# A running sum over 768 steps: one chain of six chunks or two chains of three

## The chip, the cores and the metric

The kernel runs on one core of a Trainium2 chip. The core has TensorE (matmuls into PSUM banks; "PE" in the profile, its weight loads "PEld"), VectorE ("DVE"), ScalarE ("ACT"), GpSimd ("POOL") and SyncE ("SP", which issues the DMAs here). The metric is the device time of one execution in microseconds. Before the change three runs took 821.51, 821.87 and 823.55 us, median 821.87.

## The reference

A gated linear attention feeds two dense blocks. What the change touches is in the attention:

```python
mag = sqrt(a_re**2 + a_im**2)
scale = minimum(mag, 0.999) / (mag + 1e-6)
ar, ai = a_re * scale, a_im * scale
for t in range(768):                       # per batch (4) and head (8), state 48 x 48, complex
    S_re, S_im = ar[t]*S_re - ai[t]*S_im + outer(k[t], v[t]), ar[t]*S_im + ai[t]*S_re
    y[t] = q[t] @ S_re
x = y                                      # (4, 768, 384)
u = x + (relu(x^T @ w_tok1) @ w_tok2)^T    # dense 1: over time, then over channels
x = u + relu(u @ w_ch1) @ w_ch2
k = relu(mix(x, mu_k) @ w_k); out = sigmoid(mix(x, mu_r) @ w_r) * (k*k @ w_v)   # dense 2
```

The kernel does not step through time. The product of the factors up to step t is the exponential of a running sum of logarithms (the decay) and a rotation by a running sum of angles. Both running sums over the 768 steps are what is changed here.

## The kernel before

**Tiling.** Time is cut into six chunks of 128 steps (partitions), channels are 384 wide (8 heads of 48). X1, X2 and X3 hold all six chunks of a batch in fp32. The four batches go one after the other through `attention(b)` and `dense(b)`; batch 0's attention runs alone, with weight conversions beside it, and the attention of each later batch is emitted between the dense work of the one before.

**The order of the attention** is a string of words, SEQ0 for batch 0 (L32) and SEQ1 for batch 1. S, L, A and R are squares, logarithms, slopes and angles of a half (three chunks); B is 50 warming matmuls; `C3` is `sums(3)`, the running sum of the fourth chunk; `D0` is `decays(0)`, the exponentials of the first half's sums; T0 to T7 are the steps of a software pipeline over the chunks (scaling q and k, DMA transposes, score matmuls, state update, y). In the kernel before, batch 0 has `C0 C3 C1 C4 C2 D0 C5 D1`.

**A chunk's sum** (`products`, `add`). For the decay (operand X3, PSUM tag "u") and the angle (X2, tag "y") a triangle matmul (`tri32`, fp32, 128x384) sums within the chunk. What came before the chunk is added by a carry matmul (`last32`, 32 partitions) from a copy of the last row of the chunk before, which ScalarE puts into `carry32` (the tile CH). In batch 0 the kernel before runs two chains: chunks 0 to 2, and chunks 3 to 5. The fourth chunk starts the second chain with all-ones matmuls (`ones32`) over chunks 0, 1 and 2, for each of the two sums. The second chain has a carry buffer of its own, and each chain has its own pair of PSUM banks (`bank`: ps_1 for the first, ps_a for the second). Batch 1 runs one chain through all six chunks, with one bank for each sum. Batches 2 and 3 take other matmuls.

**A chunk's evacuation** (`sums`, after the yield): two ScalarE copies that round (X1 and a scratch tile, L468 and L470), and two VectorE operations that take the remainder (`rest`, and X2, L472 and L473); both read the PSUM bank. In the profile these operations have L334, the line of the helper that calls them; the matmuls of the attention have L479.

**The decays of a half** (`decays`): two ScalarE sigmoids of 128x1152 and two VectorE multiplies of 128x1152.

**Filler.** `keep_busy` puts ten small matmuls with low priority (offset -2000) behind each of the twelve sums of batch 0 (L487); `warm` puts 50 in front of them (L495). They keep TensorE at work and compute nothing that is used.

**Weights.** `weights_gen` loads weight pieces (L253, tile wst, two buffers) and splits each into two fp16 parts: three VectorE operations to decode (L264 to L266), one to round (L269, or ScalarE's L271), one for the remainder (L275). The next piece but one is loaded when a remainder is done. Pieces have low priority in batch 0's attention (offset -300) and high in the dense part (100).

**The order on the engines.** A planner orders the instructions of each engine before the run, by priority (the place in the program, with offsets: 100 for the sums' matmuls and carry copies, `P_PE`) and by its own estimates of when operands and engines come free. Within `attention(0)`, manual edges keep ScalarE's and VectorE's work in the program's order only in the steps T0 to T7.

Of the kernel before, what the change touches and what calls it, by code (L numbers as in the profile page):

```python
# [13 lines left out]
ACTF = mybir.ActivationFunctionType  # L14
# [4 lines left out]
C = H * D  # L19
NJ = S // 128  # L20
# [8 lines left out]
PRE, CHUNKS = 29.0, 51.7  # L29


SEQ0 = "S0 L0 S1 L1 B1 A0 R0 A1 R1 C0 C3 C1 C4 C2 D0 C5 D1 T0 T1 T2 T3 T4 T5 T6 T7"  # L32
SEQ1 = "S0 S1 L0 L1 A0 R0 A1 R1 C0 C1 C2 D0 C3 C4 C5 D1 T0 T1 T2 T3 T4 T5 T6 T7"

ORD0 = "f01 f11 b0 w0 q0 k0 e0 i2 v1 u0 m01 m11 h01 h11 x2 a0 l0"
# [63 lines left out]
def split_path(  # L99
# [13 lines left out]
    def behind(later, earlier):  # L113

        for x in later:
            for y in earlier:
                tc.add_manual_dep(x.ins, y.ins.name, no_sync, reason="issue order")
        return later
# [5 lines left out]
    ACT = nc.scalar.activation  # L124
# [13 lines left out]
    tri32 = [const.tile([128, 128], F32, name=f"tri32{i}") for i in range(2)]  # L138
    ones32 = [const.tile([128, 128], F32, name=f"ones32{i}") for i in range(2)]
    last32 = const.tile([128, 128], F32, name="last32")  # L140
# [25 lines left out]
    CH = const.tile([128, 7, C], F32, name="CH")  # L166
# [4 lines left out]
    X3 = const.tile([128, NJ, C], F32, name="X3")  # L171


    carry32 = [CH[:, 5:7], CH[:, 3:5]]

    x_hl = {}

# [147 lines left out]
    def attention(b):  # L325
# [3 lines left out]
        st, hl, at = {}, {}, [None]  # L329

        def chained(fn, last):

            def call(*a, **k):
                ins = fn(*a, **k)  # L334
                if b == 0 and at[0] is not None:
                    last[:] = behind([ins], last)
                return ins

            return call

        on_act, on_dve = [], []
        ACT = chained(nc.scalar.activation, on_act)
# [10 lines left out]
        def tmp2():  # L353
            return tmps.tile([128, 512], F32, tag="tmp", name="t2")[:, 0:C]
# [4 lines left out]
        def wide():  # L359
            return one.tile([128, 3, C], F32, tag="wide", name="wide")  # L360
# [40 lines left out]
        def bank(tag, J, shape):  # L401
            if b == 0 and J % 2:
                return ps_a.tile(shape, F32, tag={"u": "a0", "y": "a1"}[tag], name=tag)
            return ps_1.tile(shape, F32, tag=tag, name=tag)


        def parts(J):
            if J < NJ and not plain:
                hl[J] = two.tile([128, 4, C], F16, tag="hl", name="hl")
                for X, k, sc in ((X3, 0, 2.0 ** L_S), (X2, 2, 2.0 ** F_S / (2.0 * math.pi))):  # L410
                    ACT(hl[J][:, k], X[:, J], ACTF.Copy, scale=sc)
                    STT(hl[J][:, k + 1], X[:, J], sc, hl[J][:, k], op0=MUL, op1=SUB)

        acc = {}

        def add(J, o, ps, X):

            k = J // 3 if b == 0 else 0
            first = J == 3 * k
            with tc.high_priority(offset=P_PE):  # L420
                if plain:
                    for i in range(J if first else 0):
                        MM(out=ps, lhsT=ones32[o // 2], rhs=X[:, i], start=i == 0, stop=False)
                    MM(out=ps, lhsT=tri32[o // 2], rhs=X[:, J], start=J == 0 or not first, stop=first)
                    if not first:
                        MM(out=ps, lhsT=last32[96:128], rhs=carry32[k][96:128, o // 2], start=False, stop=True)
                    if J + 1 < NJ and J + 1 != 3 * k + (3 if b == 0 else NJ):
                        ACT(carry32[k][96:128, o // 2], ps[96:128], ACTF.Copy)
                    return


                if J > 0:
                    for i in range(2):
                        nc.tensor.matmul(out=ps, lhsT=anti, rhs=hl[J - 1][:, o + i], start=False, stop=True, skip_group_check=True)
                for i in range(2):
                    nc.tensor.matmul(out=ps, lhsT=tri, rhs=hl[J][:, o + i], start=J == 0 and i == 0, stop=True, skip_group_check=True)
# [1 line left out]
        both = ((X3, 0), (X2, 2))  # L438

        def products(J):  # L440
            k = J // 3 if b == 0 else 0
            if J == 0 or plain:
                for o, tag in ((0, "u"), (2, "y")):
                    acc[J, o] = bank(tag, k if at[0] is None else at[0], [128, C])
            else:
                for o in (0, 2):
                    acc[J, o] = acc[J - 1, o]
            if not plain:
                if J == 0:
                    parts(0)  # L450
                parts(J + 1)
            for X, o in both:
                last_mm.clear()
                add(J, o, acc[J, o], X)
                if b == 0:
                    keep_busy(N_FILL0)

        def sums(J):

            if J == 0 or b > 0 or J % 3:  # L460
                products(J)
            if b == 0 and J == 0:
                products(3)
            if J % 3 == 0:
                rest[J // 3] = wide() if b > 0 or J == 0 else R[:, 1024:1024 + 3 * C].rearrange("p (j f) -> p j f", j=3)
            yield 0.4 if plain else 1.3
            ps = [acc.pop((J, o)) if plain else acc[J, o] for o in (0, 2)]
            ACT(X1[:, J], ps[0], ACTF.Copy, bias=ROUND_L)  # L468
            r = tmp2()
            ACT(r, ps[1], ACTF.Copy, bias=ROUND)  # L470

            STT(rest[J // 3][:, J % 3], X1[:, J], ROUND_L, ps[0], op0=SUB, op1=SUB)  # L472
            STT(X2[:, J], r, ROUND, ps[1], op0=SUB, op1=SUB)  # L473
            yield 1.2
# [3 lines left out]
        def MM(**k):  # L478
            last_mm[:] = [nc.tensor.matmul(**k)]  # L479
            if b == 0:  # L480
                behind(last_mm, ahead)

        def keep_busy(n):

            with tc.high_priority(offset=-P_FILL):
                for _ in range(n):
                    ins = nc.tensor.matmul(out=h1_ps[1][:, C:512], lhsT=tri, rhs=tri, start=False, stop=False, skip_group_check=True)  # L487
                    behind([ins], last_mm)
# [240 lines left out]
        if b == 0:  # L729
            h1_ps.extend((ps_a.tile([128, C], F32, tag="a2", name="h1a"), ps_1.tile([128, 512], F32, tag="s", name="h1b")))  # L730
            nc.tensor.matmul(out=h1_ps[1], lhsT=tri, rhs=qk16["qh"][:, 0:4], start=True, stop=True)
        kinds = {"S": squares, "L": logs, "A": slopes, "R": angles, "C": sums, "D": decays, "T": step, "B": warm}
        for word in (SEQ0 if b == 0 else SEQ1).split():
            yield from kinds[word[0]](int(word[1]))
# [186 lines left out]
    def run(gen, got, want):  # L921

        while got < want:
            c = next(gen, None)
            if c is None:
                return float("inf")
            got += c
        return got
# [18 lines left out]
    def attentions():  # L947
        for b in range(1, B):
            yield from attention(b)
            done[0] = b  # L950
            yield 0.0

    ag, acc = attentions(), 0.0
    cg, seen_w = checks_gen(), 0.0
    for b in range(B):
# [5 lines left out]
        for cost in dense(b):  # L961
# [5 lines left out]
            if b + 1 < B:  # L967
                x = pos / 141.0
                acc = run(ag, acc, lo + (hi - lo) * (x + KINK[b] * x * (1.0 - x)))
# [207 lines left out]
def fused_kernel(tc, *args):  # L1177
    nc = tc.nc

    args = [words(x) if x.dtype == I64 else x for x in args]  # L1180
    with tc.tile_pool(name="flag", bufs=1) as pool:
        flag = pool.tile([1, 1], I32, name="flag")
        raw, args = args[:14], args[14:]
        split_path(tc, *args[:4], *raw[5:14], *args[4:], flag)
        bad = nc.values_load(flag[0:1, 0:1], min_val=0, max_val=1)
        with tc.If(bad != 0):
            general_path(tc, *raw, args[4], args[7])
# [53 lines left out]
```

## Time and profile before

| | |
|---|---|
| runs shown | 821.51, 821.87, 823.55 us |
| profiled execution | 825.2 us, its span 823.4 us |
| TensorE busy | 750.1 us (91%) |
| VectorE busy | 583.5 us (71%) |
| ScalarE busy | 520.7 us (63%) |
| GpSimd busy | 21.1 us (3%) |
| granted clock, mean | 0.97 |
| chain of waits by engine | PE 51%, ACT 18%, DVE 15%, DMA 11% |

Times in the profile are microseconds from the start of the span. A row of the timeline has start, duration, engine, line, operation, output and inputs, shape, and a count where several equal instructions are merged; an fp32 matmul has two records. In brackets stands how long the engine had been idle before, and what ended that. Consecutive operations overlap a little in the records, so the step from one start to the next is the better measure of what one costs.

### The profile page before, as it was taken

The numbers are of one execution on the slowest core, as the hardware profiler recorded it, in microseconds if no ns is written. First come the engines' busy times: TensorE is split into PE (matmuls) and PEld (weight loads), VectorE is DVE, ScalarE is ACT, GpSimd is POOL, SyncE is SP. The second block draws the span as 40 slices with busy tenths as digits, with TensorE's granted clock in tenths as the row PEclk, the third lists the DMA queues.
The fourth block names the chain that finished last, engine by engine and source line by source line (L and its number), as shares of the span: only waits on it lengthen the run. The fifth ranks groups of instructions, "written<-read, shape, count | busy, mean of one in ns | idle before, by whom it ended". The sixth has DMA issues, their size and how long they took to land.

```text
span 823.4 us, 15170 instructions
## 1 busy us (share of the span) xinstructions
PE 750.1 (91%) x6107; PEld 474.0 (58%) x6107; DVE 583.5 (71%) x1016; ACT 520.7 (63%) x988; POOL 21.1 (3%) x53
## 2 busy tenths in 40 slices
PE   0969879999998999999998899999999999999996
PEld 0559855455555655556665556566565666666553
DVE  3898979999998858877667556769675534484822
ACT  6785569767767988655658696556656533142742
POOL 3000000001000000000000000000000000010000
PEclk9986989999999999999999999999999999999998
DMA  8249983444754821161407501143406432867300
GB/s 271 76 98 227 197 278 116 129 149 129 201 123 104 192 72 49 58 135 27 97 1 149 153 1 39 58 91 46 94 10 88 81 106 54 273 199 262 114 29 33
DMA packets 137949, 94.92 MB, mean 115 GB/s; under 512 B 104592, under 2 KB 120208, under 8 KB 137872
## 3 DMA queue, kind: packets, MB, share of 16 engines
q1 hardware_dynamic: 137872, 93.88, 44.6%
q8 instruction: 50, 0.82, 0.4%
q14 instruction: 27, 0.22, 0.1%
HBM read 63.97 MB, written 4.72 MB: 83 GB/s over the span
## 4 chain that ended last, share of the span: by engine, by line
PE 51%; ACT 18%; DVE 15%; DMA 11%; issue 4%; SPq 1%; ACTq 0%; DVEq 0%
PE ps L738 23%; PE a L738 16%; PE y L479 4%; ACT X L334 4%; DVE X L334 4%; PE u L479 3%; PE sp L479 2%; DMA X<-by_time_a_re_dram 2%; ACT tmp L870 2%; DMA Rc<-kl 2%; DMA Rc<-kh 1%; DVE Wc L334 1%; DMA Rc<-ql 1%; ACT ps L903 1%; ACT ps L904 1%
## 5 line engine op out<-in xcount | busy, mean ns | idle before, releaser
L738 PEld LDWEIGHTS <-wc 128*128 128x128 f16 x1728 | 166.7, 98 | 116.1 <-issue 13.5
L738 PE MATMUL a<-g,wc 128*128 128x384 f16 x864 | 162.5, 327 | 0.0
L738 PE MATMUL ps<-uh,wc 128*128 128x384 f16 x576 | 157.2, 327 | 2.3 <-DVE ul L788 1.5
L738 PE MATMUL a<-wv,g 128*128 128x384 f16 x576 | 110.2, 327 | 3.0 <-ACT g L905 2.6
L479 PEld LDWEIGHTS <-Rc 96*128 96x128 f16 (+1 forms) x1416 | 82.9, 101 | 48.8 <-issue 10.4
L738 PE MATMUL ps<-xkh,wk 128*128 128x384 f16 x384 | 107.2, 331 | 1.5 <-DVE g L906 1.5
L831 ACT ACTIVATE g<-ps 128x384 f16<-128x384 f32 x96 | 46.5, 484 | 86.5 <-PE ps L738 86.1
L738 PE MATMUL ps<-ul,wc 128*128 128x384 f16 x288 | 94.3, 327 | 0.0
L832 DVE SCALAR_TENSOR_TENSOR g<-ps,g 128x384 f16<-128x384 f32 x96 | 53.1, 555 | 45.9 <-ACT g L831 45.7
L479 PE MATMUL sp<-Rc 96*128 96x128 f16 x504 | 60.1, 228 | 18.8 <-DMA Rc<-kh 6.0
L738 PEld LDWEIGHTS <-g 128*128 128x128 f16 x576 | 54.0, 98 | 38.5 <-ACT g L905 4.8
L738 PEld LDWEIGHTS <-wk 128*128 128x128 f16 x576 | 55.4, 98 | 35.5 <-issue 4.3
L479 PE MATMUL y<-CH,Rc 96*128 96x48 f16 (+1 forms) x912 | 63.2, 185 | 4.0 <-ACT Rc L334 2.2
L738 PE MATMUL ps<-xkl,wk 128*128 128x384 f16 x192 | 63.3, 330 | 0.0
L906 DVE TENSOR_TENSOR g<-ps,g 128x384 f16<-128x384 f32 x64 | 35.5, 554 | 37.2 <-ACT g L905 37.1
L903 ACT ACTIVATE ps<-ps 128x384 f32<-128x384 f32 x64 | 30.5, 477 | 34.0 <-PE ps L738 30.8
L334 DVE TENSOR_TENSOR Wc<-cs,X 128x768 f32<-128x768 f32 x48 | 45.0, 952 | 0.2
L334 ACT ACTIVATE X<-X 128x1152 f32<-128x1152 f32 x32 | 37.0, 1158 | 11.5 <-DMA X<-by_time_a_re_dram 10.0
L334 DVE TENSOR_TENSOR m<-sp,tri 128x512 f32<-128x512 f32 x48 | 32.6, 685 | 15.1 <-PE sp L479 15.1
L479 PE MATMUL u<-CH,kh 128*128 128x48 f16 x320 | 38.5, 190 | 4.8 <-ACT kh L334 4.8
L334 ACT ACTIVATE X<-X,col_c 128x1152 f32<-128x1152 f32 x32 | 40.1, 1252 | 0.8 <-DVE Rc L334 0.4
L738 PE MATMUL ps<-wr,xrh 128*128 128x384 f16 x144 | 37.1, 325 | 0.0
(212 smaller groups left out, 1378.9 us busy)
## 6 DMA issues: line engine op xcount, KB each, us to landing
wst<-in_moe_w_ch_dram SPq DMA_DIRECT2D x24, 768.0 KB, 4.4
CH<-in_qk_dram SPq DMA_DIRECT2D x18, 384.0 KB, 3.0
wst<-in_moe_w_tok_dram SPq DMA_DIRECT2D x8, 768.0 KB, 5.0
wst<-in_moe_w_k_dram SPq DMA_DIRECT2D x8, 768.0 KB, 4.7
wst<-in_moe_w_v_dram SPq DMA_DIRECT2D x8, 768.0 KB, 4.6
X<-by_time_a_re_dram SPq DMA_DIRECT2D x8, 576.0 KB, 4.9
X<-by_time_a_im_dram SPq DMA_DIRECT2D x8, 576.0 KB, 6.7
CH<-by_time_v_dram SPq DMA_DIRECT2D x24, 192.0 KB, 3.1
```

What stands on the lines that cost most here:

```text
L334: ins = fn(*a, **k)
L479: last_mm[:] = [nc.tensor.matmul(**k)]
L738: return [nc.tensor.matmul(out=ps, lhsT=lh[a_], rhs=rh[b_], start=start and n_ == 0, stop=stop and n_ == 2) for n_, (a_, b_) in enumerate( ...
L831: ACT(part[:, 0], ps, ACTF.Relu)
L832: last_ev[:] = [STT(part[:, 1], ps, 0.0, part[:, 0], op0=MAX, op1=SUB)]
L870: ACT(w[:, 0:N], z[:, 0:N], ACTF.Copy, scale=o[:, c:c + 1])
L903: ACT(ps, ps, ACTF.Relu)
L904: ACT(ps, ps, ACTF.Square, scale=2.0 ** (SQ_S // 2 - XK_S - WK_S))
L906: last_ev[:] = [TT(part[:, 1], ps, part[:, 0], op=SUB)]
```

## The change

In batch 0 the sums of all six chunks form one chain, in the order of the chunks, as in batch 1. The all-ones matmuls and the second carry buffer go. The PSUM banks alternate by chunk (even chunks ps_1, odd chunks ps_a) and not by chain. The decays of the first half stand in the program behind the third chunk's sums and in front of the fourth's; before, they stood behind the third chunk's and in front of the sixth's. Batches 1 to 3 get the same instructions as before.

```diff
-SEQ0 = "S0 L0 S1 L1 B1 A0 R0 A1 R1 C0 C3 C1 C4 C2 D0 C5 D1 T0 T1 T2 T3 T4 T5 T6 T7"
+SEQ0 = "S0 L0 S1 L1 B1 A0 R0 A1 R1 C0 C1 C2 D0 C3 C4 C5 D1 T0 T1 T2 T3 T4 T5 T6 T7"
...
-    carry32 = [CH[:, 5:7], CH[:, 3:5]]
+    carry32 = CH[:, 5:7]
...
         def add(J, o, ps, X):

-            k = J // 3 if b == 0 else 0
-            first = J == 3 * k
             with tc.high_priority(offset=P_PE):
                 if plain:
-                    for i in range(J if first else 0):
-                        MM(out=ps, lhsT=ones32[o // 2], rhs=X[:, i], start=i == 0, stop=False)
-                    MM(out=ps, lhsT=tri32[o // 2], rhs=X[:, J], start=J == 0 or not first, stop=first)
-                    if not first:
-                        MM(out=ps, lhsT=last32[96:128], rhs=carry32[k][96:128, o // 2], start=False, stop=True)
-                    if J + 1 < NJ and J + 1 != 3 * k + (3 if b == 0 else NJ):
-                        ACT(carry32[k][96:128, o // 2], ps[96:128], ACTF.Copy)
+                    MM(out=ps, lhsT=tri32[o // 2], rhs=X[:, J], start=True, stop=J == 0)
+                    if J > 0:
+                        MM(out=ps, lhsT=last32[96:128], rhs=carry32[96:128, o // 2], start=False, stop=True)
+                    if J + 1 < NJ:
+                        ACT(carry32[96:128, o // 2], ps[96:128], ACTF.Copy)
                     return
...
         def products(J):
-            k = J // 3 if b == 0 else 0
             if J == 0 or plain:
                 for o, tag in ((0, "u"), (2, "y")):
-                    acc[J, o] = bank(tag, k if at[0] is None else at[0], [128, C])
+                    acc[J, o] = bank(tag, J, [128, C])
...
         def sums(J):

-            if J == 0 or b > 0 or J % 3:
-                products(J)
-            if b == 0 and J == 0:
-                products(3)
+            products(J)
             if J % 3 == 0:
```

## Rows read from the trace of the kernel before

**Rows 1.** The page, part 1: busy time, share of the span, instructions.

```profile
PE 750.1 (91%) x6107; PEld 474.0 (58%) x6107; DVE 583.5 (71%) x1016; ACT 520.7 (63%) x988; POOL 21.1 (3%) x53
```

**Rows 2.** Stretches: length, then PE, PEld, DVE, ACT, POOL busy, granted clock, DMA.

```profile
25.00:50.00 25.00, 25.00 (x160) 15.50 (x159) 23.23 (x38) 19.74 (x37) 0.00 (x0) 1.00 0.32 96
50.00:70.00 20.00, 13.67 (x150) 12.34 (x148) 20.00 (x30) 12.44 (x26) 0.00 (x0) 0.60 0.78 169
70.00:80.00 10.00, 9.46 (x114) 8.86 (x114) 7.26 (x12) 5.29 (x9) 0.00 (x0) 0.61 1.12 222
...
140.00:260.00 120.00, 113.90 (x790) 64.46 (x789) 114.62 (x200) 91.09 (x179) 3.73 (x10) 1.00 0.50 136
```

**Rows 3.** The chain of waits: start, length, engine, what; 10 to 150 us.

```profile
39.77 0.56 DVE X L334
...
48.34 2.41 DVE X L334 x3
...
105.56 8.09 DMA wst<-in_moe_w_ch_dram
```

**Rows 4.** Timeline of TensorE, 25 to 52 us.

```profile
25.10 1.59 PE L479 MATMUL y<-X,tri 128*128 128x384 f32 x2
26.49 0.90 PE L479 MATMUL y<-X,ones 128*128 128x384 f32 x2
...
31.09 0.81 PE L479 MATMUL y<-X,tri 128*128 128x384 f32 x2
...
33.77 0.91 PE L479 MATMUL y<-CH,last 32*128 32x384 f32 x2
...
40.45 0.80 PE L479 MATMUL y<-CH,last 32*128 32x384 f32 x2
41.19 0.91 PE L479 MATMUL y<-X,tri 128*128 128x384 f32 x2
...
42.68 0.91 PE L479 MATMUL y<-CH,last 32*128 32x384 f32 x2
...
44.16 1.01 PE L495 MATMUL h1b<-warm,tri 128*128 128x128 f16 x15
45.01 6.86 PE L487 MATMUL h1b<-tri 128*128 128x128 f16 x120
```

**Rows 5.** Timeline of ScalarE, 34 to 47 us.

```profile
34.77 0.48 ACT L334 ACTIVATE CH<-y 32x384 f32<-32x384 f32 x1 [0.82 <-PE y L479]
...
41.17 1.26 ACT L334 ACTIVATE X<-X,col_c 128x1152 f32<-128x1152 f32 x1
...
42.43 0.47 ACT L334 ACTIVATE t<-y 128x384 f32<-128x384 f32 x1
...
44.27 0.49 ACT L334 ACTIVATE X<-u 128x384 f32<-128x384 f32 x1
...
45.02 1.26 ACT L334 ACTIVATE X<-X,col_c 128x1152 f32<-128x1152 f32 x1
```

**Rows 6.** Timeline of VectorE, 42 to 51 us.

```profile
42.27 0.96 DVE L265 SCALAR_TENSOR_TENSOR wf<-wst,wf 128x768 int32<-128x768 int32 x1
...
43.61 2.62 DVE L334 SCALAR_TENSOR_TENSOR X<-wide,X 128x1152 f32<-128x1152 f32 x2
46.15 0.55 DVE L334 SCALAR_TENSOR_TENSOR Rc<-X,u 128x384 f32<-128x384 f32 x1
...
47.08 2.62 DVE L334 SCALAR_TENSOR_TENSOR X<-Rc,X 128x1152 f32<-128x1152 f32 x2
49.61 1.14 DVE L334 SCALAR_TENSOR_TENSOR X<-qk,col_c,X 128x384 f32<-128x384 f32 x2
```

**Rows 7.** Timelines of VectorE and TensorE, around 114 us.

```profile
113.67 0.56 DVE L264 TENSOR_SCALAR wf<-wst 128x768 int32<-128x768 int32 x1 [3.86 <-DMA wst<-in_moe_w_ch_dram]
...
114.81 0.32 PE L738 MATMUL h1a<-xl,wt 128*128 128x384 f16 x1 [3.21 <-DVE xl L334]
```

**Rows 8.** Waits from 115 to 205 us: who for whom, total, times, longest.

```profile
PE u L479 <- DVE wide L334: 0.4, 1, 0.4
```

## The prediction

> **What bounds the kernel now.** The page comes first: TensorE is busy for 750.1 us of the 823.4 us span, 91% [rows 1]. That is an average, and the change touches one stage only, the running sums of batch 0, so the second view is the table of stretches. From 25 to 50 us, where the sums lie, TensorE shows no gap, VectorE is busy 23.23 us of 25.00, and the granted clock is 1.00; from 50 to 70 us VectorE is busy 20.00 of 20.00 and TensorE 13.67; from 140 to 260 us TensorE is busy 113.90 of 120.00 [rows 2]. So VectorE carries the start and TensorE the dense part behind it. What the start gains reaches the end as long as the dense part begins that much earlier: its matmuls are a fixed amount of work.
>
> The third view is the chain of waits. It leaves the sums before they end: at 39.77 it comes to a VectorE evacuation, and from there to the three pieces at 48.34 every piece of work is VectorE's [rows 3]. The reader is to see that TensorE, full as it looks, does not end this stage alone: VectorE's queue does, and it holds weight conversions (0.96 us at 42.27, for example, [rows 6]) beside the sums.
>
> **The matmuls.** The sums start at 25.10 and the last matmul of them gives way to filler at 44.16 [rows 4]: 19.06 us for 26 matmuls. Six of these go away, the all-ones ones by which the fourth chunk rebuilt the sum of three chunks. They and one triangle matmul among them stand from 26.49 to 31.09: seven in 4.60, so 0.66 each and 3.95 for six. Two carry matmuls of the fourth chunk are added; two take 1.48 (42.68 to 44.16). The four triangle matmuls of the second and fourth chunk ran in one row, 31.09 to 33.77, 0.67 each; in a chain each alternates with carry matmuls, where four matmuls take 2.97 (41.19 to 44.16), 0.74 each: 0.30 more. Sum: -3.95 + 1.48 + 0.30 = -2.17, rounded to **-2.15 us** [rows 4].
>
> Does the chain itself keep up? A carry matmul of 0.91 starts at 33.77, its copy runs on ScalarE from 34.77 for 0.48 [rows 4, 5]; so the next carry matmul of that chain may start at about 35.3, 1.5 us after the one before. A chunk's four matmuls take 2.97, and the two chains (decay and angle) alternate, so one chain's turn hides under the other's matmuls. Banks alternate by chunk after the change, so a triangle matmul waits for the chunk two back: last matmul, carry copy 0.48, evacuation copy 0.49, VectorE 0.55 [rows 5, 6], in all 1.5 us and some hand-over, against 3 us until the bank is wanted. The second carry buffer falls away at no cost, since only one chain is left. Batch 1 already runs this single chain, with one bank per quantity, and there one triangle matmul waited 0.4 us for a VectorE evacuation [rows 8]. Batches 1 to 3 compute as before.
>
> **The carry copies.** Two more on ScalarE, 0.48 each [rows 5]. They are hidden: ScalarE is busy 19.74 us of 25.00 in this stretch [rows 2].
>
> **The decays of the first half.** Now the last chunk's first VectorE evacuation starts at 46.15, though its input copy ended at 44.76 (44.27 + 0.49): the decay multiplies of the first half, 2.62 us from 43.61, stand in front of it [rows 5, 6]. With these done earlier the tail is ScalarE's: the copies of the sums from 44.27, the sigmoid at 45.02, ended at 46.28, then the two multiplies of the second half, 2.62 together, from about 46.3 instead of 47.08 [rows 5, 6]. **-0.80 us**.
>
> What it costs to have them in front: two sigmoids of 1.26 each (41.17 to 42.43 with what belongs to it), 2.5 us of ScalarE, and the 2.62 of VectorE, between the third chunk's evacuations and the fourth's. In the trace a sigmoid at 41.17 held back the copy of the angle sums to 42.43, though its matmul (0.80 from 40.45) had ended at 41.25 [rows 4, 5]: 1.2 us late, and nobody waited for it. After the change the sixth chunk's triangle matmuls want the fourth chunk's bank. By the periods above the second chunk's matmuls start at about 27.2 and the fifth chunk's end at 39.1. If both sigmoids and the fifth chunk's carry copies stand in front of the fourth chunk's copies, these run at 39.6 and 40.1, VectorE frees the first bank at 40.7, and TensorE waits 1.6. If the sigmoids fall into ScalarE's gaps, nothing. Below nothing is excluded for this item alone, since the gain of moving them is already counted. I take **+0.5**, nearer to nothing, because ScalarE has 5.26 us of idle in 25.00. The Trainium skill (PSUM — Partial Sum Buffer, Engine vs sequencer instructions) says that the ScalarE and VectorE queues are strict FIFO, which speaks against this change: by it alone a carry copy or an evacuation behind a sigmoid waits for all of it, and the sum would take the 1.6 in place of the 0.5. The late copy at 42.43 agrees with the rule [rows 5].
>
> **What is behind it on VectorE.** The sums' stretch would so end 2.95 - 0.5 = 2.45 us sooner, but VectorE's work in it stays: 23.23 us busy, 1.77 idle [rows 2]. At least 0.7 us of it, so one weight operation (0.96, as at 42.27 [rows 6]), must go behind the stretch, where VectorE has no idle until 70 us. Bounds: nothing, if it lands in the 2.74 us of idle between 70 and 80 or later [rows 2]; 2.9, if three such operations move in front of the steps of the first chunks. I take **+1.0**, one operation, the least that the balance wants. The moved decays issue no DMA, and no queue of SP or POOL is passed by them.
>
> **Further on.** At 105 to 115 us the last chunk's low half of x (VectorE) stands behind a weight conversion that waits 3.86 for its DMA; TensorE waits 3.21 for that x [rows 7]. The chain of waits goes through that DMA, 8.09 us from 105.56 [rows 3]. It is issued when an earlier weight piece is finished and shares the engines with batch 1's first loads, which move with the attention steps. I count it at nothing: these loads come earlier, and the piece that releases the weight DMA comes later by the displaced operation. Bounds: -3.2, if the order flips and x goes first; +1.0, if the DMA slips by an operation. The granted clock is 0.60 in 50 to 70 us and 0.61 in 70 to 80 [rows 2]; the filler (120 records from 45.01, 6.86 us) moves with the sums, and I expect the same gap behind it.
>
> **The sum:** -2.15 - 0.80 + 0.5 + 1.0 = -1.45 us. The profiled execution took 825.2, with a span of 823.4 and 1.8 around it; it would become 823.75. It lies 3.3 above the median of the runs shown, 821.87, to which the same difference gives **820.4**.
>
> **Rivals.** A: all of it arrives. The planner puts the decays into ScalarE's gaps and the displaced weight operation behind 70 us: -2.95, so 818.9, and down to 815.7 if x is no longer held by the weight DMA (-3.2). For it: 5.26 us of idle on ScalarE, 2.74 on VectorE behind 70 us. Against it: 20.00 of 20.00 on VectorE before that [rows 2].
>
> B: nothing arrives, since VectorE is what ends last: the chain of waits is on VectorE from 39.77 on [rows 3], and the 2.95 are filled by three weight operations that now stand at 25 to 42 us. 821.9, from 821.4 to 823.
>
> C: slower. With two chains TensorE never ran dry, so all 120 filler matmuls and 15 of the warming ones stood behind the sums. With one chain the planner may see TensorE wait for a carry and put filler into the chain, where a matmul of the sums then waits behind it. A filler costs 0.057 (6.86 over 120), the 15 cost 0.85 (44.16 to 45.01) [rows 4]. All of them inside: 7.7 us, so -2.95 + 7.7 = +4.75, 826.6. With one weight operation displaced as well (+1.0) it turns slower from (2.95 - 1.0) / 0.057 = 34 fillers on, and measurably so from 78. For it: a sigmoid of 1.26 in front of a carry. Against it: 1.5 us of turn under 2.97 of matmuls.
>
> **How the numbers follow.** A measurement of this kernel tells about 0.3% from no change, 2.5 us: under 819.4 is faster, over 824.3 slower. Forecast 0.38 (819.4 to 821.4), A 0.30, B 0.17, C 0.15. So faster 0.30, same 0.55, slower 0.15. The range goes from 817.0 (it leaves out the part of A with the flipped order) to 824.8 (it leaves out most of C).
>
> **What would show it.** Sums from 25.1 to about 42.0 in 22 matmuls, none of them all-ones; the first step's multiply (49.61 now) at 47.2; the decay multiplies of the first half before the last chunk's evacuation. A gap on TensorE before the sixth chunk is the bank wait; fillers between triangle and carry matmuls are C; weight operations between 47 and 68 in greater number than now are B; x of the last chunk no longer behind a weight DMA is A. The prediction is wrong if the first step starts within 1 us of now, or if the dense part, whose first matmul of that late x is at 114.81 [rows 7], starts otherwise than the first step moves.

## The result, and the profile after

The changed kernel takes 833.01 us (median of 4 runs, 829.96 to 836.09) where the kernel before takes 822.71 beside it: ratio 1.0117, 95% interval 1.0077 to 1.0158. It is slower by some 10 us, outside the range. The profiled execution took 832.92, its span 831.1.

The stage that the change touches became shorter all the same. The first fence is TensorE's timeline there (columns as in [rows 4]).

```profile
24.84 0.94 PE L471 MATMUL y<-X,tri 128*128 128x384 f32 x2
...
29.13 1.01 PE L487 MATMUL h1b<-warm,tri 128*128 128x128 f16 x15
...
37.33 0.28 PE L479 MATMUL h1b<-tri 128*128 128x128 f16 x2
...
41.96 0.80 PE L471 MATMUL y<-CH,last 32*128 32x384 f32 x2
42.70 6.71 PE L479 MATMUL h1b<-tri 128*128 128x128 f16 x117
```

The sums give way to filler at 42.70, 1.46 us sooner than in [rows 4]; 0.26 of that is an earlier start. Inside the chain stand the 15 warming matmuls and three fillers. On VectorE the attention's first step starts sooner too. `Wc` is its first product; the first line is the kernel before, the others are the kernel after.

```profile
52.07 1.82 DVE L334 TENSOR_TENSOR Wc<-cs,X 128x768 f32<-128x768 f32 x2
```

```profile
44.06 1.36 DVE L334 SCALAR_TENSOR_TENSOR X<-Rc,X 128x1152 f32<-128x1152 f32 x1
...
45.80 1.35 DVE L334 SCALAR_TENSOR_TENSOR X<-Rc,X 128x1152 f32<-128x1152 f32 x1
...
49.07 1.82 DVE L334 TENSOR_TENSOR Wc<-cs,X 128x768 f32<-128x768 f32 x2
```

So the first step is 3.0 us ahead. The last low half of x, which in the kernel before stood behind a weight conversion waiting for its DMA [rows 7], comes at 108.33 where it came at 114.14, and the dense part's first relu (of 160; a relu is the ScalarE operation that empties a matmul's bank into the tile g) is at 123.56 where it was at 130.27: **6.7 us ahead**. At the fifth relu the kernel after is 3.3 us behind, at the 25th 7.4, at the last 7.7. The table of stretches shows it (columns as in [rows 2]): to the first relu, to the fifth, to the 25th, to the last; the first line of each fence covers the whole way from 24.90 to the 25th. Before, then after:

```profile
24.90:236.37 211.47, 192.65 (x1555) 126.23 (x1553) 195.14 (x315) 148.92 (x265) 3.73 (x10) 0.93 0.62 161
50.00:130.27 80.27, 65.50 (x754) 53.88 (x752) 70.78 (x108) 50.30 (x88) 0.00 (x0) 0.81 0.86 201
130.27:140.60 10.33, 9.98 (x58) 5.62 (x57) 8.96 (x14) 10.30 (x15) 0.00 (x0) 1.00 0.36 116
140.60:236.37 95.77, 92.06 (x589) 51.13 (x587) 92.07 (x157) 68.48 (x129) 3.73 (x10) 1.00 0.52 150
236.37:812.05 575.68, 549.49 (x4501) 341.67 (x4499) 373.86 (x679) 352.92 (x705) 9.27 (x27) 0.99 0.38 95
```

```profile
24.90:243.74 218.84, 191.51 (x1593) 121.81 (x1591) 195.27 (x314) 151.46 (x270) 3.48 (x9) 0.93 0.62 157
50.00:123.56 73.56, 57.69 (x719) 47.79 (x720) 61.78 (x94) 46.12 (x80) 0.00 (x0) 0.86 0.88 191
123.56:143.93 20.37, 17.71 (x88) 9.05 (x87) 18.37 (x28) 17.94 (x27) 0.00 (x0) 1.00 0.46 148
143.93:243.74 99.81, 91.70 (x607) 50.23 (x605) 92.25 (x158) 65.80 (x123) 3.48 (x9) 0.95 0.57 158
243.74:819.77 576.03, 548.94 (x4450) 340.24 (x4450) 373.16 (x680) 350.82 (x701) 9.91 (x28) 0.99 0.39 94
```

Two things are to be seen. The stretch from the first relu to the fifth doubles, 10.33 to 20.37. And VectorE's work up to the 25th relu is the same, 195.14 and 195.27 us; the stretch is that work plus VectorE's idle time, 16.33 before (211.47 - 195.14) and 23.57 after. The idle grew by 7.24, the stretch by 7.37. That is a balance and not yet a cause. By the same rows the idle grew by 0.46 before 50 us, 2.29 from there to the first relu, 0.63 to the fifth and 3.86 behind it, so more than half of the growth stands late. What VectorE did not do before the first relu (70.78 to 61.78) it does right behind it (8.96 to 18.37).

What it did not do is weight conversion. The next view groups VectorE's weight operations in front of the first `Wc` (count, busy us and mean ns of one), before and after:

```profile
L266 DVE SCALAR_TENSOR_TENSOR wst<-wst,wf 128x768 int32<-128x768 int32 x3 | 2.9, 955 | 0.0
L265 DVE SCALAR_TENSOR_TENSOR wf<-wst,wf 128x768 int32<-128x768 int32 x3 | 2.9, 954 | 0.0
L275 DVE SCALAR_TENSOR_TENSOR wt<-wst,wt 128x768 f16<-128x768 f32 x3 | 2.9, 951 | 0.0
L264 DVE TENSOR_SCALAR wf<-wst 128x768 int32<-128x768 int32 x3 | 1.7, 565 | 0.0
```

```profile
L275 DVE SCALAR_TENSOR_TENSOR wt<-wst,wt 128x768 f16<-128x768 f32 x2 | 1.9, 966 | 0.0
L265 DVE SCALAR_TENSOR_TENSOR wf<-wst,wf 128x768 int32<-128x768 int32 x2 | 1.9, 966 | 0.0
L266 DVE SCALAR_TENSOR_TENSOR wst<-wst,wf 128x768 int32<-128x768 int32 x2 | 1.9, 960 | 0.0
L264 DVE TENSOR_SCALAR wf<-wst 128x768 int32<-128x768 int32 x2 | 1.1, 568 | 0.0
```

Four operations fewer, one of each kind, 3.43 us in all by their means before the change (0.955 + 0.954 + 0.951 + 0.565). That is more than the 3.0 us by which the first step came sooner: **the gain at the first step is weight work put off** (one_chain_weights_in_front, below, tests it). In the steps behind it the order holds about one weight operation for each step of some 8 us, so four operations are four steps. VectorE's timeline shows the remainder of the fourth piece (L275), at 57.08 in the kernel before, at 93.79 in the kernel after:

```profile
57.08 0.95 DVE L275 SCALAR_TENSOR_TENSOR wt<-wst,wt 128x768 f16<-128x768 f32 x1
```

```profile
76.89 0.55 DVE L269 TENSOR_SCALAR wt<-wst 128x768 f16<-128x768 f32 x1
...
92.05 1.82 DVE L334 TENSOR_TENSOR Wc<-cs,X 128x768 f32<-128x768 f32 x2
93.79 0.95 DVE L275 SCALAR_TENSOR_TENSOR wt<-wst,wt 128x768 f16<-128x768 f32 x1
```

A remainder frees the buffer for the load of the next piece but one. SyncE's queue and VectorE's idle times in the kernel after:

```profile
99.34 0.57 SPq L716 DMA_DIRECT2D X<-by_time_a_re_dram  x1
99.96 1.35 SPq L716 DMA_DIRECT2D X<-by_time_a_im_dram  x1
...
103.14 1.11 SPq L253 DMA_DIRECT2D wst<-in_moe_w_ch_dram  x2
```

```profile
108.33 0.62 DVE L334 SCALAR_TENSOR_TENSOR xl<-y,col_c,xh 128x384 f16<-128x384 f32 x1 [2.77 <-ACT xh L334]
110.44 1.36 DVE L334 TENSOR_TENSOR X<-X,wide 128x1152 f32<-128x1152 f32 x1 [1.48 <-ACT wide L334]
```

Two weight loads stand behind batch 1's first loads, and VectorE idles for most of 105 to 110, with no landed piece to convert. By the view of DMA issues from 99 to 115 us these two land 10.2 us after their issue (median):

```profile
wst<-in_moe_w_ch_dram SPq DMA_DIRECT2D x2, 768.0 KB, 10.2
```

The kernel before idles there about as long, 3.86 us in front of its own late load [rows 7], but by then it has converted two pieces more (remainders at 104.57 and 108.84). The remainders of the sixth and the ninth piece on VectorE, before and then after, are 17.7 and 13.3 us apart:

```profile
104.57 0.95 DVE L275 SCALAR_TENSOR_TENSOR wc<-wst,wc 128x768 f16<-128x768 f32 x1
...
126.31 0.96 DVE L275 SCALAR_TENSOR_TENSOR wc<-wst,wc 128x768 f16<-128x768 f32 x1
```

```profile
122.27 0.96 DVE L275 SCALAR_TENSOR_TENSOR wc<-wst,wc 128x768 f16<-128x768 f32 x1 [1.24 <-ACT wc L271]
...
139.63 0.97 DVE L275 SCALAR_TENSOR_TENSOR wc<-wst,wc 128x768 f16<-128x768 f32 x1
```

The dense part then outruns its weights. ScalarE rounds a part of the eighth piece at 132.03, and TensorE's timeline shows who waits:

```profile
132.03 0.90 ACT L271 ACTIVATE wc<-wst 128x768 f16<-128x768 f32 x1
```

```profile
129.81 1.63 PE L730 MATMUL a<-g,wc 128*128 128x384 f16 x9
132.98 1.15 PE L730 MATMUL a<-g,wc 128*128 128x384 f16 x6 [1.55 <-ACT wc L271]
134.03 0.91 PE L471 MATMUL y<-X,tri 128*128 128x384 f32 x2
```

Behind it stand sums of batch 1 in TensorE's order (134.03), and the fifth relu, whose matmuls use the ninth piece, comes at 143.93. Late weights go on from there: between the fifth and the 25th relu TensorE's weight loads wait for ScalarE's and VectorE's parts of pieces, and the list of waits of the kernel before has neither line in that stretch (who for whom: total, times, longest).

```profile
PEld L730 <- ACT wc L271: 4.1, 3, 1.8
PEld L730 <- DVE wc L275: 2.1, 4, 0.8
```

### The profile page after: what moved, and what is told of

Its sections match the earlier page's. It is cut to its first block, busy times and chain, and to the rows that moved or that the text cites. A ratio compares the mean times of both kernels' runs of the same rounds, so it can differ in the third digit from the quotient of the medians.

```text
span 831.1 us, 15165 instructions
## 1 busy us (share of the span) xinstructions
PE 748.7 (90%) x6099; PEld 468.4 (56%) x6099; DVE 583.2 (70%) x1016; ACT 521.4 (63%) x990; POOL 21.5 (3%) x53
## 4 chain that ended last, share of the span: by engine, by line
PE 53%; ACT 17%; DVE 16%; DMA 9%; issue 4%; SPq 1%; ACTq 0%; DVEq 0%
PE ps L730 24%; PE a L730 17%; PE y L471 4%; ACT X L334 4%; DVE X L334 4%; PE u L471 3%; DMA X<-by_time_a_re_dram 2%; PE sp L471 2%; ACT tmp L862 2%; DMA Rc<-ql 2%; DVE Wc L334 2%; DMA CH<-in_qk_dram 1%; ACT ps L895 1%; ACT ps L896 1%; DVE g L824 1%
## 5 line engine op out<-in xcount | busy, mean ns | idle before, releaser
L730 PE MATMUL ps<-uh,wc 128*128 128x384 f16 x576 | 159.2, 331 | 4.5 <-DVE ul L780 1.8
L471 PE MATMUL sp<-Rc 96*128 96x128 f16 x504 | 62.3, 230 | 24.4 <-DMA Rc<-kh 11.9
```

The costliest lines, as they stand in the source:

```text
L730: return [nc.tensor.matmul(out=ps, lhsT=lh[a_], rhs=rh[b_], start=start and n_ == 0, stop=stop and n_ == 2) for n_, (a_, b_) in enumerate( ...
```

## The experiments

Each line of the table is one kernel: median and number of runs, ratio to the kernel before beside it with its interval, and from the profiled execution the first relu, the stretch to the fifth, the stretch from 24.90 to the 25th with VectorE's work in it.

| kernel | us (runs) | ratio | first relu | to 5th | to 25th | VectorE |
|---|---|---|---|---|---|---|
| before, beside | 822.71 (4), 823.9 (19), 822.7 (26), 823.1 (23) | 1 | 130.27 | 10.33 | 211.47 | 195.14 |
| after | 833.01 (4) | 1.0117 [1.0077, 1.0158] | 123.56 | 20.37 | 218.84 | 195.27 |
| one_chain_again | 834.28 (6) | 1.0137 [1.0109, 1.0165] | 121.90 | 20.39 | 215.74 | 194.81 |
| hold_two_chains | 833.33 (4) | 1.0115 [1.0031, 1.0199] | 123.87 | 20.39 | 217.94 | 194.70 |
| one_chain_weights_in_front | 826.74 (9) | 1.0049 [1.0026, 1.0071] | 132.00 | 10.35 | 213.38 | 194.94 |
| two_chains_decays_early | 823.43 (10) | 1.0006 [0.9985, 1.0028] | 130.16 | 10.36 | 211.05 | 194.57 |
| one_chain_decays_late | 826.71 (10) | 1.0047 [1.0007, 1.0087] | 126.25 | 17.02 | 213.68 | 188.12 |
| one_chain_round_on_act | 826.36 (10) | 1.0031 [0.9996, 1.0066] | 128.48 | 10.86 | 211.98 | 194.10 |
| one_chain_round_half | 825.83 (12) | 1.0033 [1.0003, 1.0064] | 125.05 | 11.55 | 209.12 | 188.23 |
| two_chains_round_on_act | 833.35 (4) | 1.0123 [1.0047, 1.0198] | 134.31 | 10.34 | 217.00 | 197.27 |
| two_chains_round_on_act_behind_x | 827.79 (12) | 1.0047 [1.0025, 1.0069] | 131.17 | 9.58 | 212.36 | 193.07 |
| two_chains_weights_behind_x | 825.65 (12) | 1.0038 [1.0017, 1.0060] | 128.31 | 9.57 | 209.70 | 195.28 |
| one_chain_weights_both | 831.52 (6) | 1.0109 [1.0078, 1.0139] | 134.57 | 9.58 | 216.63 | 196.59 |
| one_chain_weights_early | 838.86 (6) | 1.0170 [1.0137, 1.0203] | 145.47 | 11.42 | 229.04 | 203.12 |

**hold_two_chains.** The weights late without the chain: the kernel before, with the third piece's last decode operation held behind the first half's decays (`behind(a, b)` makes the instructions a wait for b).

```diff
+            if i == 2:
+                held.append(op)               # op: the decode operation of L266
...
+            if b == 0 and k == 0:
+                behind(held, [last])          # last: the second multiply of decays(0)
```

> The kernel before, two chains untouched, with one edge more: the third decode operation of weight piece 2 is issued behind the decay multiplies of the first half. So about four weight operations fewer stand in front of the first step, as in the changed kernel. Theory W (the loss is late weights: what is pushed out of the sums' stretch comes back at one operation per attention step, and the dense part waits for it): dense part of batch 0 starts some us earlier than before, then a jump of about 12 us at the channel matmuls of f = 4; in all 829 to 834 us. Rival C1 (the loss comes from the single chain, its banks or its carries): 820 to 824 us, no jump.

It takes 833.33, as theory W said; with four runs the interval is wide, 0.3 to 2.0%. The two chains are untouched, and the trace shows what the kernel after shows: the double load, TensorE's wait, the stretch of 20.39. The edit adds lines above, so L271 is L275 here.

```profile
102.19 1.91 SPq L255 DMA_DIRECT2D wst<-in_moe_w_ch_dram  x2
```

```profile
133.29 1.15 PE L744 MATMUL a<-g,wc 128*128 128x384 f16 x6 [1.54 <-ACT wc L275]
```

So the order of the weight work is enough for the loss, and the chain isn't needed for it. It is enough for the early start as well: the first relu is at 123.87, 6.4 us ahead of the kernel before, with none of the sums' matmuls taken away.

**one_chain_weights_in_front.** The other direction: the changed kernel, with the first step's product held behind the decode of the fourth piece, which puts as many weight operations in front of it as in the kernel before (the third piece's remainder still stands later, 49.15 against 40.24).

```diff
+            if i == 3:
+                held.append(op)
...
+            if b == 0 and J == 0 and nm == "q":
+                behind([ins], held)           # ins: the first product Wc
```

> The changed kernel with one issue-order edge: the first step's first product on VectorE stands behind the third decode operation of weight piece 3. So 15 weight operations stand in front of the first step, as in the kernel before, and 11 of them no longer. Chain, banks and decays as changed. Theory W (late weights are the whole loss): no jump in the dense part, 819 to 824 us, 8 to 13 us below the changed kernel. Rival C1 (the chain or its banks cost something by themselves): 828 to 833 us.

826.74, between the two ranges expected: six of the ten us come back, and the long stretch is gone:

```profile
132.00:142.35 10.35, 9.95 (x58) 5.63 (x57) 8.98 (x14) 10.32 (x16) 0.00 (x0) 1.00 0.34 113
```

The second half's decay multiplies still end early (the next operation starts at 47.15; 49.61 before), but the first `Wc` is at 52.49 (before 52.07): with the weight work back in front nothing of the 3.0 us is left. A rest of 0.49% stays against the kernel before. In the profile 1.7 us of it are there at the first relu; the profiled execution was the slowest of its nine, so the rest can't be placed.

**two_chains_decays_early** and **one_chain_decays_late** take the two parts of the change apart. The first is the kernel before with `D0` in front of the fifth chunk's sums, the second the changed kernel with `D0` behind them.

```diff
-... C0 C3 C1 C4 C2 D0 C5 D1 ...
+... C0 C3 C1 C2 D0 C4 C5 D1 ...
```

```diff
-... C0 C1 C2 D0 C3 C4 C5 D1 ...
+... C0 C1 C2 C3 C4 D0 C5 D1 ...
```

> The kernel before with only the decays moved: behind the first chain's end and in front of the fifth chunk's sums; two chains as before. The weight operations keep their places. Theory W: 821 to 825 us, the same as before within 0.3%. Rival C2 (the decays' place costs): 828 to 833 us.

> The changed kernel with the decays of the first half where they were, in front of the sixth chunk's sums; chain and banks as changed. Theory W: as few weight operations stand in front of the first step, so the weights are as late: 829 to 835 us. Rival C2 (the decays' new place pushes the weights out or holds the chain): 819 to 824 us.

Earlier decays with two chains: no change (1.0006). One chain with late decays: the weights come as late as in the changed kernel (the sixth piece's remainder at 120.87; 122.27 after, 104.57 before), and yet it loses less than half as much; 826.71 lies in neither of the two ranges expected. By the 25th relu VectorE has done 188.12 us of work, 7 less than in the kernel before: other work of batch 1 was put behind that point. So lateness alone does not fix the price; what else the queues hold does.

**one_chain_round_on_act, one_chain_round_half.** The changed kernel with VectorE relieved: the rounding of each piece's parts (four on VectorE, L269) goes to ScalarE in whole or in half.

```diff
-N_DVE, WBITS = 4, 0x38000000
+N_DVE, WBITS = 0, 0x38000000   # and 2
```

> The changed kernel, with the rounding of weight pieces 0 to 3 (0.56 us each on VectorE) moved to ScalarE, so four VectorE operations fewer before the steps. Theory W: pieces 5 and 6 are done at about 105 us again, no jump in the dense part, 814 to 822 us. Rival C1: stays at 830 to 835 us. Rival C2 (the decays' new place is what costs): stays at 830 to 835 us.

> One chain, rounding of two weight parts of each piece on ScalarE that VectorE did (two in place of four on VectorE): half the dose of one_chain_round_on_act. The fourth and the fifth piece now stand one step earlier than in the changed kernel and one step later than in the kernel before. Theory W: a time between 826.4 (all on ScalarE) and 833 us, about 828 to 830, with a jump at the seventh relu eviction of about half of 12 us. Rival (the chain itself): 832 to 834 us.

826.36, short of the 814 to 822 expected, and 825.83: the half dose, expected between, does as much as the whole. The whole gives the weights back in time (sixth piece at 102.86, seventh at 109.64; 108.84 before). The half does so for the sixth (106.19) but not for the seventh (118.69), and the jump that was expected of it is there: from the first relu to the seventh it takes 24.29 us, where the kernel before takes 16.86 and the kernel after 29.14. It starts 5.2 us ahead of the kernel before, loses that again, and is no faster than it.

**two_chains_round_on_act, two_chains_round_on_act_behind_x.** The same relief for the kernel before; and once more with the eighth and later pieces' first operation behind the last low half of x.

```diff
+            behind([TS(f, hi, ...)], x_last if phase[0] and i >= 7 else ())
```

> The control of the run before: the kernel before with the same rounding on ScalarE. Theory W: the weights were not late there, so little changes, 818 to 824 us, and the gap between the two kernels with the rounding on ScalarE is the pure worth of the single chain, 2 to 4 us in its favour. Rival C1: this one is faster than the single chain by some 10 us, as without the edit.

> Two chains, all rounding of weights on ScalarE, and the weight pieces from the eighth on start on VectorE only behind the last low half of x. If the 833 us of two_chains_round_on_act came from the weight operation that stood 4.97 us at the head of VectorE's queue, waiting for its DMA in front of the last x, this takes it away: the dense part starts 4 to 6 us sooner than there, and the time falls to 823 to 827 us. If it came from ScalarE's rounding itself, the time stays above 830.

The first, expected at 818 to 824, takes 833.35. A part of that is the opposite mistake: pieces come early in VectorE's order, and one waits for its DMA at the head of the queue, in front of the last steps.

```profile
108.41 0.56 DVE L264 TENSOR_SCALAR wf<-wst 128x768 int32<-128x768 int32 x1 [4.97 <-DMA wst<-in_moe_w_ch_dram]
```

It is the wait of [rows 7], grown from 3.86. With x first the first relu comes 3.1 us sooner (4 to 6 were expected), and the time falls from 833.35 to 827.79, just above the 823 to 827 expected. That is 5.6 of the 9.5 us over the kernel before; no run shows where the rest comes from.

**two_chains_weights_behind_x, one_chain_weights_both.** That edge alone on the kernel before, and both edges on the changed one.

> The kernel before with one issue-order edge: from weight piece 7 on, the decode stands on VectorE behind the last chunk's low half of x. In the kernel before, piece 7 waits 3.86 us for its DMA in front of that x. If that wait is a cost of its own, the dense part starts 3 us earlier and the total falls by 2 to 3 us, 820 to 822 us; if the dense part waits for weights anyway, the gain comes back as a wait for piece 7 or 8 and the total stays within 1 us.

> Both edges on the changed kernel: weights in front of the first step as before, and from piece 7 on behind the last x. Theory W: the best of the four, 816 to 821 us, if the 3 us of the x wait are real; otherwise as the run with the first edge alone.

In the kernel before it takes the wait of [rows 7] away; the first relu comes 2.0 us sooner, and 12 runs are 0.38% slower, not faster. Both edges together, 831.52 where 816 to 821 were expected: the first relu is 4.3 us late. More fixed order was no cure; why the two add up so badly stays open.

**one_chain_weights_early.** The changed kernel with the weights' priority in the attention raised.

```diff
-P_W = (-300, 100)
+P_W = (-100, 100)
```

> One chain, with the weight pieces of batch 0's attention put forward (offset -100 in place of -300): seven more weight operations in front of the last step's product than before. Theory W with its other side (a weight operation in front of a step costs its own length on the start): no piece comes late, no jump at the seventh relu eviction, but the dense part starts some 5 us later than in the kernel before (7 operations of about 0.8 us), so 826 to 829 us. A rival: the order on VectorE does not matter and the single chain costs the 10 us: 832 to 834 us. Another: early pieces are a gain, under 822 us.

838.86, 10 more than expected, and all of it is there at the start: the first relu is 15.2 us late, the last 15.5. The way to the seventh relu, where no jump was expected, takes 23.21 us (16.86 before).

```profile
24.90:253.94 229.04, 198.72 (x1591) 132.01 (x1589) 203.12 (x326) 154.92 (x276) 4.41 (x10) 0.89 0.62 155
```

```profile
83.40 0.56 DVE L264 TENSOR_SCALAR wf<-wst 128x768 int32<-128x768 int32 x1 [1.75 <-DMA wst<-in_moe_w_ch_dram]
...
90.34 0.56 DVE L264 TENSOR_SCALAR wf<-wst 128x768 int32<-128x768 int32 x1 [2.40 <-DMA wst<-in_moe_w_ch_dram]
...
118.65 0.56 DVE L264 TENSOR_SCALAR wf<-wst 128x768 int32<-128x768 int32 x1 [2.58 <-DMA wst<-in_moe_w_ch_dram]
```

The expectation counted the operations in front of the steps (seven of some 0.8 us) and left out the loads that they wait for, 6.7 us in these three rows; the remaining part of the 15.2 isn't placed.

**one_chain_again.** The changed kernel unedited.

> The changed kernel once more, unedited, to see which of its late losses come back. Theory W (weight pieces late in the dense part, because four weight operations lost their place in front of the first step): around 1.011 of the time before; the jump of some 12 us between the fourth and the seventh relu eviction of the dense part comes back, since it hangs on the order of the instructions. The extra loss of about 4 us around 620 us, where TensorE waited 5.44 us for a transpose, need not come back if it belongs to one execution. If the clock carries a part: the mean granted clock of these runs lies under that of the kernel before by about 0.005 to 0.01, as in the first four runs (0.969 against 0.977).

834.28. The stretch to the fifth relu comes back to 0.02 us. The way to the 25th is 215.74, so VectorE's idle time in it is 20.93, 4.6 more than before, where the first execution had 7.24: its size differs between executions. TensorE's wait for a transpose around 620 us is there again too, 2.6 us in both executions (1.0 in the kernel before; 5.44 was the length of the transpose in the chain of waits).

None of these kernels beats the kernel before.

## Why the prediction was wrong

**The matmuls and the decays were about right.** The sums took 19.06 us and take 17.86. Inside stand 15 warming matmuls and three fillers, 1.28 us by their steps, which the sum left to rival C; without them the 22 matmuls take 2.48 less, against 2.15 forecast; 0.61 of it lies in the first matmul, whose step is 1.39 before and 0.78 after and which the sum left alone. The +0.5 for a wait on a bank measured nothing: no such wait shows before the sixth chunk. The ScalarE queue in order, on which the bound of 1.6 rested, made a carry copy about 0.75 us late once (its matmul ended at 36.01, the copy ran behind a sigmoid at 36.76), and TensorE didn't stand still for it. So the last matmul moved by 1.46 against 2.15 - 0.5 = 1.65, with errors that cancel. The second half's decay multiplies end 2.54 sooner (49.61, then 47.07), against 2.95 - 0.5 = 2.45.

**The first step agrees by luck.** It moved by 3.0, against 2.95 in case A. But that gain is put-off weight work: in one_chain_weights_in_front, with matmuls and decays as changed, the first `Wc` is 0.4 later than before. The multiply that the prediction meant to watch (49.61) can't be used as its sign: it is one of a pair that the kernel after starts at 39.10 and 41.71, inside the sums.

**"Further on" went to its bound.** The x wait, counted at nothing with a bound of -3.2, fell away: the order flipped, and the dense part came 6.7 us sooner, against 2.95 + 3.2 = 6.15 with that bound. Up to the first relu case A's number held, but not its reason, since hold_two_chains has a lead of 6.4 without the chain. The prediction had named a dense part that moves otherwise than the first step as a sign of being wrong; 6.7 against 3.0 is that sign.

**The step that failed is "What is behind it on VectorE".** It took one displaced weight operation, priced it at its own length (+1.0), and let it act on the first steps. Four were displaced, the first step gained from that, and their price came some 80 us later and was not their length but some 10 us: the order gives back one per step, each remainder releases a load, the loads fell behind batch 1's, VectorE ran dry, and the dense part waited for weights. hold_two_chains shows that such an order alone makes 9.4 us with two chains, one_chain_weights_in_front that 6.3 of the changed kernel's 10.3 go when the operations are put back. How the loss divides between the waits for weights and what they bring with them was not separated.

**Under it lies a false reading of [rows 2].** From 140 to 260 us it shows TensorE busy for 113.90 of 120 and VectorE for 114.62. The prediction read the first number, called the dense part a fixed amount of matmuls, and concluded that what the start gains reaches the end. VectorE was at least as full. Up to the 25th relu VectorE does the same work before and after, 195.14 and 195.27 us: the change took matmuls away and moved decays. By this balance a gain at that point needs less idle time of VectorE (16.3 us of 211.5), or work put behind it (188.12 us in one_chain_decays_late), while a new order could raise the idle time. Rival B had this reason, "VectorE is what ends last", but ended its sum at the stage's border, with nothing gained; that the balance can be negative was not in it. The slower rival, C, was about another mechanism.

**What stays open.** The 0.3 to 0.5% that one chain costs with the weights in time (one_chain_weights_in_front, one_chain_round_half, one_chain_round_on_act), and the unequal price of equal lateness in one_chain_decays_late. So is the slowness that stays in two_chains_round_on_act_behind_x. The profiled executions differ by 7 to 7.7 us between before and after, the medians by 10 to 11: the execution profiled of the kernel before lies 2.5 above its median.

## What to carry to other kernels

Where two engines are both near full in a stretch, add up each one's work from the start of the change to the end of that stretch: an edit that removes no work from the fuller one can only win there by lowering its idle time or by putting work behind the stretch, and an event that comes earlier may be work put off. When a planner orders the queues, a few displaced background operations are priced by what they release (a buffer, a load, a due date far behind), not by their length. An operation that converts loaded data has two wrong places, too late for its user and so early that it waits for its load at the head of its queue; the first cost some 10 us here, the second some 6 in one kernel (833.35 against 827.79), while taking a wait of 3.86 out of the kernel before gained nothing.

## What was not expected of the hardware

Executions of one kernel spread more than the three runs shown at first: those of the kernel before, 68 in three comparisons, from 817.2 to 828.4. The longer ones have the lower mean granted clock: over the nine to twelve runs of each of seven of the kernels above, 0.01 of mean clock goes with 4 to 7 us (3 to 4 in the kernel before). The kernel before has a mean of 0.977, the changed kernel 0.969 over its 10 runs. In its trace the clock is below full in a place where the kernel before keeps it (220 to 230 us; before, then after), in the stretch in which TensorE waited 1.76 us for VectorE:

```profile
220.00:230.00 10.00, 9.56 (x95) 5.72 (x95) 9.77 (x18) 7.70 (x13) 0.00 (x0) 1.00 0.76 197
```

```profile
220.00:230.00 10.00, 7.82 (x56) 4.58 (x57) 8.03 (x13) 2.53 (x4) 0.00 (x0) 0.66 0.94 259
```

A mean of 0.66 is time at both levels, 1.2 and 2.4 GHz. From the fifth relu to the 25th the mean granted clock is 0.95 to 0.98 in the traces of the four kernels whose sixth remainder starts at 120 us or later (the changed kernel twice, hold_two_chains, one_chain_decays_late), and 1.00 in the ten others. Part of the loss may be such clock behind late weights; no run here holds the one and changes the other.
